# Values of the first eight sub-blocks as 64x64x64 products, and one copy for their transposed probabilities

## The chip, the cores and the metric

The kernel runs on one core of a Trainium2 chip. The metric is device time in microseconds. The engines are TensorE (PE in the profile; its weight loads are PEld), VectorE (DVE), ScalarE (ACT), GpSimd (POOL) and SyncE (SP), which issues most of the DMAs.

## The reference

Attention within chunks of 64 tokens, with 8 heads of 64, then a feed-forward layer (FFN) with a leaky relu whose slope alpha is learned per hidden unit. All of it is float32; the products of the FFN are made from a high and a low part of each operand.

```
q, k, v: (8, 8, 576, 64); chunks of 64 tokens
scores = q_c @ k_c^T / 8;  attn = softmax(scores)     # 64 x 64 per chunk and head
x = (attn @ v_c) as (4608, 512)
h = x @ w_in                                          # (4608, 2048)
g = max(h, 0) + alpha * min(h, 0)
out = g @ w_out                                       # (4608, 512)
```

## The kernel before

The 4608 tokens are 36 sub-blocks of 128 (two chunks of 64), and 9 blocks of 512. The FFN runs over blocks; the first three are computed plainly, the others in pairs with fewer products. Attention runs ahead of the FFN, a sub-block at a time, on the same engines.

The first eight sub-blocks (`s < EARLY`) make the x of blocks 0 and 1 and have a form of their own. The scores of a sub-block are eight products, one for each head, over both chunks at once: the keys stand block-diagonally in a tile with zeros elsewhere (`kbds`). A score tile has 128 partitions (the parity of the head, then 64 queries) and 512 columns (head pair, chunk, key).

- `attn_softmax` takes the maxima (L210, L212 on VectorE), eight exponentials with their sums (L217, ScalarE) and divides (L219 to L221, VectorE).
- `attn_transpose` makes four TensorE transposes of 128x128 (L245) into one PSUM bank. Its rows are then chunk and key, its columns head and query. Two ScalarE copies (L252, L253), of 64 rows each, bring chunk 0's rows into the first half and chunk 1's into the second half of a tile `pbds[s % 4]`. The other halves hold zeros, set once by eight memsets on GpSimd (L97), so the tile is block-diagonal by chunk.
- `attn_values` makes eight products (L263), one for each head: 128 rows of v by 64 columns, against 128 columns of the block-diagonal tile. They fill one bank `xo`.
- `attn_x` copies `xo` to `xh` (L295, ScalarE, rounded to the high part) and subtracts for `xl` (L296, VectorE). `done_x[s]` remembers the subtraction; the split of some weights is issued behind it.

From sub-block 8 on, scores and values are products of 64x64x64 (L194, L275), which lie on four tiles of the array and write two banks, and x comes out of these in two halves of 256 columns (L300, L301, or L291).

`attn_psum(s, n)` gives the PSUM bank: for s < 6, bank n = 1 (transposes) is `ps_o0` or `ps_o2`, bank n = 2 (values) is `ps_o1` or `ps_o3`, by the parity of s. Otherwise it is one of the two banks named `ps_a`, which all scores use too. The four `ps_o` banks later hold the FFN's second product.

The order of work: sub-blocks 0 to 3 go through scores, transpose and values as a pipeline of three stages before the FFN begins; sub-blocks 4 to 7 are written beside its first two steps. Each step is `ffn_in` for one of 16 slices f of the hidden units (L314, then L304 to L306 for the leaky relu and L326, L327 for the two parts of g) and, a step later, `ffn_out` (L339). Block 0 takes f = 0 to 2, block 1 f = 0 to 8, then each the rest; meanwhile the weights of one f after another are split into high and low parts (L130 to L138, ScalarE and VectorE). What each engine does in which order is fixed at build time by a planner that keeps dependences, has its own costs for the instructions, and prefers attention and the leaky relu (`high_priority`). A bank is given to its next user when its last reader is done.

Of the kernel before, what the change touches and what calls it, by code (L numbers as in the profile page):

```python
# [12 lines left out]
ALU = mybir.AluOpType  # L13
# [14 lines left out]
def tile_local_attention_prelu_ffn(  # L28
# [12 lines left out]
    nc = tc.nc  # L41
    P = 128
    NSUB, C = qT.shape[1], 64
    DM = out.shape[1]
    NT = NSUB * 128
    H = DM // C
# [3 lines left out]
    NP = H // 2  # L50
    SCALE = 1.0 / float(C) ** 0.5
    TB = 512
    SPB = TB // P
# [4 lines left out]
    EARLY = 2 * SPB  # L58
# [14 lines left out]
    def f32(t):  # L73
        return t.bitcast(F32)
# [4 lines left out]
    def room(n, shape):  # L79
        side, f = ("wi", NF - 1 - n // 2) if n % 2 else ("wo", NF - 1 - n // 2)  # L80
        return const.tile(shape, F32, name=f"{side}{f}")

    NBD = 4
    kbds = [room(n, [P, 2, H, C]) for n in range(NBD)]
    pbds = [room(NBD + n, [P, 2, H, C]) for n in range(NBD)]
    qs = [room(2 * NBD + n, [P, 2, H, C]) for n in range(2)]
    prs = [room(2 * NBD + 2 + n, [P, 2, H, C]) for n in range(2)]
    vs = [room(2 * NBD + 4 + n, [P, 2, DM]) for n in range(2)]
# [3 lines left out]
    for n in range(NBD):  # L92
        for c in range(2):
            (nc.vector if n == 0 else nc.gpsimd).memset(kbds[n][(1 - c) * C:(2 - c) * C, c], 0.0)
    for n in range(NBD):
        for c in range(2):
            nc.gpsimd.memset(pbds[n][(1 - c) * C:(2 - c) * C, c], 0.0)  # L97

    ident = const.tile([P, P], F32, name="ident")
    make_identity(nc, ident)  # L100
# [4 lines left out]
    def pe(ins):  # L105

        return tc.keep_in_program_order(ins) if pinned[0] else ins
# [39 lines left out]
    att = []  # L147
# [5 lines left out]
    pdiag = {}  # L153
# [12 lines left out]
    def attn_psum(s, n):  # L166
        if s < SPB + 2 and n:
            t = 2 * (s % 2) + n - 1
            return ps_o.tile([P, 512], F32, name=f"ps_o{t}")
        return ps_a.tile([P, 512], F32, name="ps_a")  # L170
# [70 lines left out]
    def attn_transpose(s):  # L241
        pr = probs.pop(s)
        tp = attn_psum(s, 1)
        for hp in range(NP):
            pe(nc.tensor.transpose(  # L245
                tp[:, hp * P:(hp + 1) * P],
                pr[:, 2 * hp:2 * hp + 2, :].rearrange("p c k -> p (c k)"),
                ident,
            ))
        tp3 = tp.rearrange("p (g k) -> p g k", k=C)  # L250
        pbd = pbds[s % NBD]
        nc.scalar.copy(pbd[0:C, 0], tp3[0:C])  # L252
        nc.scalar.copy(pbd[C:2 * C, 1], tp3[C:2 * C])  # L253
        pdiag[s] = pbd

    def attn_values(s):
        v_sb = qkv.pop(s)[2]
        p = pdiag.pop(s)
        if s < EARLY:
            xo = attn_psum(s, 2)  # L260
            for h in range(H):
                par, hp = h % 2, h // 2
                pe(nc.tensor.matmul(  # L263
                    xo[par * C:(par + 1) * C, hp * P:(hp + 1) * P],
                    lhsT=v_sb[:, h * C:(h + 1) * C],
                    rhs=p[:, :, h],
                    start=True, stop=True,
                ))
            return xo.rearrange("p (g t) -> p g t", t=P)

        for hp in range(NP):
            for par in range(2):
                for c in range(2):
                    h, rows = 2 * hp + par, slice(c * C, (c + 1) * C)
                    pe(nc.tensor.matmul(  # L275
                        att[c][par * C:(par + 1) * C, hp * C:(hp + 1) * C],
                        lhsT=v_sb[rows, h * C:(h + 1) * C],
                        rhs=p[rows, :, par * NP + hp],
                        start=True, stop=True,
                    ))  # L280
        return [a[:, :NP * C].rearrange("p (g t) -> p g t", t=C) for a in att]

    done_x = {}

    def attn_x(s, xo):
        sl = slice((s % SPB) * P, (s % SPB + 1) * P)
        if s >= PLAIN * SPB:

            for c in range(2):
                at = slice((s % SPB) * P + c * C, (s % SPB) * P + (c + 1) * C)  # L290
                nc.scalar.copy(x[s // SPB][:, :, at], xo[c])  # L291
            return
        xh, xl = x[s // SPB]
        if s < EARLY:
            nc.scalar.copy(xh[:, :, sl], xo)  # L295
            done_x[s] = nc.vector.tensor_tensor(xl[:, :, sl], xo, f32(xh[:, :, sl]), op=ALU.subtract)  # L296
            return
        for c in range(2):
            at = slice((s % SPB) * P + c * C, (s % SPB) * P + (c + 1) * C)
            nc.scalar.copy(xh[:, :, at], xo[c])  # L300
            nc.vector.tensor_tensor(xl[:, :, at], xo[c], f32(xh[:, :, at]), op=ALU.subtract)  # L301

    def prelu(g, h, f):
        nc.scalar.activation(g, h, AF.Relu, scale=-1.0)  # L304
# [85 lines left out]
    def attend(part, s):  # L390
        with tc.high_priority(offset=HIGH):
            if part == 0:
                attn_softmax(s, attn_scores(s))
            elif part == 1:
                attn_transpose(s) if s < EARLY else attn_blocks(s)
            else:
                attn_x(s, attn_values(s))

    def visit(old, new):

        att[:] = [ps_a.tile([P, TB], F32, name="ps_a") for _ in range(2)]
        with tc.high_priority(offset=HIGH):
            if old is not None:
                xo = attn_values(old)
            if new is not None:
                sc3 = attn_scores(new)
                if new + 1 < NSUB:

                    attn_load(new + 1, "q", nc.scalar)
                attn_load(new, "v")  # L410
            if new is not None:
                attn_softmax(new, sc3)
            if old is not None:
                attn_x(old, xo)
            if new is not None:
                attn_blocks(new)
# [194 lines left out]
    banks = ["ps_o0", "ps_o1", "ps_o2", "ps_o3", "ps_h", "ps_h"]  # L611
# [247 lines left out]
    for pair in range(NPAIR):  # L859
# [4 lines left out]
        g = {}  # L864
# [49 lines left out]
```

## Time and profile before

| | |
|---|---|
| median of 3 runs | 835.87 us (834.64 to 837.24) |
| the profiled execution | 835.71 us |
| its span, first to last instruction | 833.9 us |
| TensorE busy | 804.0 us, 96% |
| VectorE busy | 669.6 us, 80% |
| ScalarE busy | 548.0 us, 66% |
| GpSimd busy | 215.4 us, 26% |
| mean granted TensorE clock | 0.998 |

Busy time is the union of an engine's instructions; neighbours on one engine overlap by a little, so the time from one start to the next is often less than an instruction's own duration. In the rows below a line of the timeline is: start, length, engine, line of the kernel, operation, output and inputs by name, shape, count, and in brackets the idle time before it and what ended it. "wi" and "wo" are names of SBUF tiles: before the weights need them, these tiles hold the attention's early operands, so `ACT wo<-ps_a` is an exponential or a copy out of PSUM and not a weight.

### The profile page before, as it was taken

The numbers are of one execution on the slowest core, as the hardware profiler recorded it, in microseconds if no ns is written. First come the engines' busy times: TensorE is split into PE (matmuls) and PEld (weight loads), VectorE is DVE, ScalarE is ACT, GpSimd is POOL, SyncE is SP. The second block draws the span as 40 slices with busy tenths as digits, with TensorE's granted clock in tenths as the row PEclk, the third lists the DMA queues.
The fourth block names the chain that finished last, engine by engine and source line by source line (L and its number), as shares of the span: only waits on it lengthen the run. The fifth ranks groups of instructions, "written<-read, shape, count | busy, mean of one in ns | idle before, by whom it ended". The sixth has DMA issues, their size and how long they took to land.

```text
span 833.9 us, 15382 instructions
## 1 busy us (share of the span) xinstructions
PE 804.0 (96%) x5248; PEld 642.6 (77%) x5248; DVE 669.6 (80%) x1240; ACT 548.0 (66%) x1420; POOL 215.4 (26%) x340
## 2 busy tenths in 40 slices
PE   4799999999999999999999999999999999999998
PEld 3577888777777778778778787787887888888886
DVE  6899999987788886677779996777789965668875
ACT  5986676657666776677886555777665546566452
POOL 4006223224244431111112242111122412121232
PEclk9999999999999999999999999999999999999999
DMA  9629778657698768688876799886557995555788
GB/s 287 206 77 344 236 243 266 199 162 209 200 254 216 247 211 262 214 258 270 263 240 209 225 252 329 256 274 199 192 196 242 244 300 184 188 191 187 235 230 231
DMA packets 73966, 192.40 MB, mean 231 GB/s; under 512 B 11664, under 2 KB 19104, under 8 KB 73760
## 3 DMA queue, kind: packets, MB, share of 16 engines
q0 software_dynamic: 38272, 127.43, 49.1%
q1 hardware_dynamic: 27248, 48.91, 18.5%
q10 hardware_dynamic: 8368, 15.08, 5.7%
q8 instruction: 42, 0.69, 0.3%
q14 instruction: 36, 0.29, 0.1%
HBM read 135.27 MB, written 42.99 MB: 214 GB/s over the span
## 4 chain that ended last, share of the span: by engine, by line
PE 73%; DVE 8%; DMA 7%; ACT 6%; SPq 3%; issue 3%; ACTq 0%; DVEq 0%; POOL 0%
PE ps_o L626 17%; PE ps_o L759 14%; PE ps_h L759 12%; PE ps_h L314 9%; PE ps_o L339 9%; PE ps_h L626 8%; SPq L235 3%; DMA v_sb<-v 2%; DMA pT<-t 2%; PE ps_a L275 1%; ACT pr L217 1%; DMA wi<-kT 1%; PE ps_a L194 1%; ACT wo L217 1%; DVE gl L327 1%
## 5 line engine op out<-in xcount | busy, mean ns | idle before, releaser
L339 PE MATMUL ps_o<-wo,gh 128*128 128x512 f32 x384 | 114.5, 396 | 0.6 <-ACT more L369 0.6
L314 PE MATMUL ps_h<-xh,wi 128*128 128x512 f32 x384 | 107.0, 401 | 1.8 <-DVE g L306 1.7
L314 PEld LDWEIGHTS ps_h<-xh,wi 128*128 128x128 f32 x384 | 71.8, 190 | 20.1 <-DVE g L306 2.6
L339 PEld LDWEIGHTS ps_o<-wo,gh 128*128 128x128 f32 x384 | 71.6, 188 | 18.1 <-ACT more L369 1.0
L339 PE MATMUL ps_o<-wo,gl 128*128 128x512 f32 x192 | 69.3, 396 | 0.4 <-DVE gl L327 0.4
L626 PE MATMUL ps_o<-wi,raw 128*128 128x512 f32 x171 | 67.9, 397 | 0.0
L217 ACT ACTIVATE pr<-ps_a,mx 128x64 f32<-128x64 f32 x224 | 67.4, 327 | 0.6
L626 PE MATMUL ps_o<-wo,raw 128*128 128x512 f32 x171 | 67.8, 396 | 0.0
L314 PE MATMUL ps_h<-xl,wi 128*128 128x512 f32 x192 | 52.6, 395 | 0.0
L326 ACT CAST gh<-g 128x512 fp32r<-128x512 f32 x48 | 29.8, 621 | 29.3 <-DVE g L306 27.4
L217 ACT ACTIVATION_READ_ACCUMULATOR pr<-ps_a,mx 128x1 f32 x224 | 48.9, 218 | 0.0
L564 POOL DMA_DIRECT2D raw<-wi_a x42 | 22.4, 535 | 102.1 <-PE ps_o L626 61.7
L304 ACT ACTIVATE wo<-gh 128x512 f32<-128x512 f32 x24 | 15.2, 634 | 51.1 <-DVE gh L649 51.1
L582 ACT CAST gh<-wi 128x512 fp32r<-128x512 f32 x45 | 28.0, 623 | 25.2 <-PE ps_o L759 10.9
L564 POOL DMA_DIRECT2D raw<-wo_a x42 | 22.4, 534 | 84.7 <-PE ps_o L759 43.9
L339 PEld LDWEIGHTS ps_o<-wo,gl 128*128 128x128 f32 x192 | 35.9, 188 | 9.6 <-DVE gl L327 0.8
L314 PEld LDWEIGHTS ps_h<-xl,wi 128*128 128x128 f32 x192 | 36.0, 188 | 8.5
L304 ACT ACTIVATE g<-ps_h 128x512 f32<-128x512 f32 x48 | 29.3, 611 | 18.3 <-PE ps_h L314 16.9
L626 PE MATMUL ps_o<-wi,wo 128*128 128x512 f32 x99 | 39.3, 397 | 0.0
L626 PE MATMUL ps_o<-wo,wo 128*128 128x512 f32 x99 | 39.1, 395 | 0.0
L626 PEld LDWEIGHTS ps_o<-wo,raw 128*128 128x128 f32 x171 | 32.2, 188 | 7.7
L626 PEld LDWEIGHTS ps_o<-wi,raw 128*128 128x128 f32 x171 | 32.1, 188 | 7.6
(252 smaller groups left out, 2280.9 us busy)
## 6 DMA issues: line engine op xcount, KB each, us to landing
raw<-wi_a POOLq DMA_DIRECT2D x42, 512.0 KB, 4.8
raw<-wo_a POOLq DMA_DIRECT2D x42, 512.0 KB, 4.1
wi<-wi_a POOLq DMA_DIRECT2D x21, 512.0 KB, 4.5
wo<-wi_a POOLq DMA_DIRECT2D x21, 512.0 KB, 4.8
wi<-wo_a POOLq DMA_DIRECT2D x21, 512.0 KB, 3.8
wo<-wo_a POOLq DMA_DIRECT2D x21, 512.0 KB, 4.3
v_sb<-v SPq DMA_DIRECT2D x28, 256.0 KB, 4.5
pT<-t SPq DMA_DIRECT2D x224, 32.0 KB, 3.9
```

The source lines that it names most:

```text
L194: pe(nc.tensor.matmul(att[par][c * C:(c + 1) * C, (NP + hp) * C:(NP + hp + 1) * C], lhsT=q_sb[rows, 2 * hp + c], rhs=kb[rows, 2 * hp + c], ...
L217: last = nc.scalar.activation(pr[:, g], one, AF.Exp, bias=mx[:, g], scale=SCALE, accum_out=sm[:, g])
L235: nc.sync.dma_start(out=pT[dst, i].rearrange("p h t -> p (h t)"), in_=tb[src, j].rearrange("p h t -> p (h t)"),)
L275: pe(nc.tensor.matmul(att[c][par * C:(par + 1) * C, hp * C:(hp + 1) * C], lhsT=v_sb[rows, h * C:(h + 1) * C], rhs=p[rows, :, par * NP + hp ...
L304: nc.scalar.activation(g, h, AF.Relu, scale=-1.0)
L314: pe(nc.tensor.matmul(hps, lhsT=wi[f][:, l, k * P:(k + 1) * P], rhs=xx[:, k], start=(i == 0 and k == 0), stop=(i == 2 and k == NK - 1),))
L326: nc.scalar.copy(gh, g)
L339: pe(nc.tensor.matmul(o, lhsT=a[:, ts], rhs=wo[f][:, l], start=(f == first and i == 0), stop=(f == last and i == 2),))
L564: streamed[0] = nc.gpsimd.dma_start(out=f32(t), in_=units[side][n])
L582: hi = nc.scalar.copy(t_hi, t)
L626: pe(nc.tensor.matmul(ps, lhsT=w[:, l, k * P:(k + 1) * P], rhs=xx[:, xl], start=first and at == 0, stop=at == n - 1, skip_group_check=not ...
L759: pe(nc.tensor.matmul(ps[m], lhsT=w[:, l, m * P:(m + 1) * P], rhs=xx, start=i != 6 and j == 0 and n == 0, stop=j == JF - 1 and n == 2, ski ...
```

## The change

For the first eight sub-blocks, the transposed probabilities leave PSUM in one copy of 128 rows by 512 columns, into the first half of the same tile, which is no longer block-diagonal; the eight memsets go. The values become sixteen products of 64x64x64, as in the later sub-blocks: chunk c takes 64 rows of v and of the probabilities, and writes to a bank of its own. The two banks are n = 2 as before and n = 1, the one that held the transposes. x is then made in two halves, one for each chunk, by the same lines as in the later sub-blocks of the first three blocks; `done_x[s]` is the second half's subtraction.

```
-    pbds = [room(NBD + n, [P, 2, H, C]) for n in range(NBD)]
+    pTs = [room(NBD + n, [P, 2, H, C]) for n in range(NBD)]
...
-    for n in range(NBD):
-        for c in range(2):
-            nc.gpsimd.memset(pbds[n][(1 - c) * C:(2 - c) * C, c], 0.0)
...
-        tp3 = tp.rearrange("p (g k) -> p g k", k=C)
-        pbd = pbds[s % NBD]
-        nc.scalar.copy(pbd[0:C, 0], tp3[0:C])
-        nc.scalar.copy(pbd[C:2 * C, 1], tp3[C:2 * C])
-        pdiag[s] = pbd
+        pT = pTs[s % NBD][:, 0]
+        nc.scalar.copy(pT, tp.rearrange("p (h t) -> p h t", t=C))
+        pdiag[s] = pT
...
-        if s < EARLY:
-            xo = attn_psum(s, 2)
-            for h in range(H):
-                par, hp = h % 2, h // 2
-                pe(nc.tensor.matmul(
-                    xo[par * C:(par + 1) * C, hp * P:(hp + 1) * P],
-                    lhsT=v_sb[:, h * C:(h + 1) * C],
-                    rhs=p[:, :, h],
-                    start=True, stop=True,
-                ))
-            return xo.rearrange("p (g t) -> p g t", t=P)
+        early = s < EARLY
+
+        banks = [attn_psum(s, n) for n in (2, 1)] if early else att

         for hp in range(NP):
             for par in range(2):
                 for c in range(2):
                     h, rows = 2 * hp + par, slice(c * C, (c + 1) * C)
                     pe(nc.tensor.matmul(
-                        att[c][par * C:(par + 1) * C, hp * C:(hp + 1) * C],
+                        banks[c][par * C:(par + 1) * C, hp * C:(hp + 1) * C],
                         lhsT=v_sb[rows, h * C:(h + 1) * C],
-                        rhs=p[rows, :, par * NP + hp],
+                        rhs=p[rows, h] if early else p[rows, :, par * NP + hp],
                         start=True, stop=True,
                     ))
-        return [a[:, :NP * C].rearrange("p (g t) -> p g t", t=C) for a in att]
+        return [a[:, :NP * C].rearrange("p (g t) -> p g t", t=C) for a in banks]
...
-        if s < EARLY:
-            nc.scalar.copy(xh[:, :, sl], xo)
-            done_x[s] = nc.vector.tensor_tensor(xl[:, :, sl], xo, f32(xh[:, :, sl]), op=ALU.subtract)
-            return
         for c in range(2):
             at = slice((s % SPB) * P + c * C, (s % SPB) * P + (c + 1) * C)
             nc.scalar.copy(xh[:, :, at], xo[c])
-            nc.vector.tensor_tensor(xl[:, :, at], xo[c], f32(xh[:, :, at]), op=ALU.subtract)
+            done_x[s] = nc.vector.tensor_tensor(xl[:, :, at], xo[c], f32(xh[:, :, at]), op=ALU.subtract)
```

More of the change, by code (lines that the diff above doesn't have):

```diff
@@ L275, in attn_values @@
                     pe(nc.tensor.matmul(
-                        att[c][par * C:(par + 1) * C, hp * C:(hp + 1) * C],
+                        banks[c][par * C:(par + 1) * C, hp * C:(hp + 1) * C],
                         lhsT=v_sb[rows, h * C:(h + 1) * C],
-                        rhs=p[rows, :, par * NP + hp],
+                        rhs=p[rows, h] if early else p[rows, :, par * NP + hp],
                         start=True, stop=True,
                     ))
-        return [a[:, :NP * C].rearrange("p (g t) -> p g t", t=C) for a in att]
+        return [a[:, :NP * C].rearrange("p (g t) -> p g t", t=C) for a in banks]
     done_x = {}
     def attn_x(s, xo):
-        sl = slice((s % SPB) * P, (s % SPB + 1) * P)
         if s >= PLAIN * SPB:
```

## The prediction

> **What bounds the kernel now.** I read the page's busy shares first, then a table by stage, then the chain of work inside the stage that the change touches.
>
> ```profile
> PE 804.0 (96%) x5248; PEld 642.6 (77%) x5248; DVE 669.6 (80%) x1240; ACT 548.0 (66%) x1420; POOL 215.4 (26%) x340
> ```
>
> Over the whole span TensorE (PE) is the bound, but the first eight sub-blocks lie in the first 62 us, so the stages decide. The columns after the stretch are its length, then the busy time of each engine.
>
> ```profile
> core 0: us, PE busy (x) PEld busy (x) DVE busy (x) ACT busy (x) POOL busy (x), PEclk, DMA share, GB/s
> 13.67:36.76 23.09, 14.05 (x172) 10.67 (x168) 19.89 (x49) 22.90 (x101) 0.00 (x0) 0.97 0.84 265
> 36.76:62.00 25.24, 25.24 (x150) 19.53 (x151) 22.00 (x48) 20.67 (x61) 0.00 (x0) 0.96 0.25 83
> 62.00:80.00 18.00, 16.81 (x73) 13.29 (x72) 17.84 (x36) 11.27 (x20) 12.09 (x17) 1.00 0.95 334
> 80.00:140.00 60.00, 60.00 (x260) 48.38 (x259) 57.03 (x117) 38.69 (x66) 15.95 (x21) 1.00 0.79 254
> ```
>
> There are four stages with four different bounds. From 13.67 us to the first matmul of the FFN at 36.76 us ScalarE (ACT) is busy 22.90 of 23.09 us. From there to 62 us PE never stops. From 62 to 80 us VectorE (DVE) is full, 17.84 of 18.00, and PE has its only gap. After 80 us PE is full again, so a microsecond won there is kept. The chain that ends at the first FFN matmul says the same of the first stage:
>
> ```profile
> 16.57 0.59 ACT wo L252
> ...
> 17.17 0.59 ACT wo L253
> ...
> 17.78 2.48 ACT wi L217 x16
> ...
> 36.76 0.79 PE ps_h L314
> ```
>
> Every step of it up to 36.7 us is ACT: the exponentials (L217), the two copies that bring transposed probabilities into the diagonal blocks (L252, L253), the copy that makes xh (L295), and the weights' casts. What ACT no longer does there, PE starts earlier.
>
> **The change part by part.**
>
> *One copy for two (ACT, on the path).* A pair of 64x512 copies becomes one copy of 128x512. The same columns pass per partition, only more partitions. How much the pairs hold before and after 36.76 us:
>
> ```profile
> 13.67:36.76 23.09, 2.96 (x5) 0.97 0.84 265
> 13.67:36.76 23.09, 2.91 (x5) 0.97 0.84 265
> L369 ACT COPY wo<-ps_o 128x512 f32<-128x512 f32 x2 | 1.2, 606 | 0.0
> ```
>
> The first row is L252 alone, the second L253 alone: five pairs (sub-blocks 0 to 4) lie before the FFN's start. The third is the nearest row to the new copy, 128x512 from PSUM at 0.606 us; it takes what one 64-row copy takes (2.96 / 5 = 0.59). So each pair saves about 0.58 us; five save 2.96 + 2.91 - 5 x 0.606 = 2.84 us on the path. The other three pairs lie in the stage where ACT has 4.6 us to spare and are worth nothing directly.
>
> *xh in two halves (ACT, on the path).* One 128x512 cast becomes two of 128x256. Later blocks already do this:
>
> ```profile
> 30.34 0.64 ACT L295 CAST xh<-ps_o 128x512 fp32r<-128x512 f32 x1
> 30.81 0.60 ACT L252 COPY wi<-ps_o 64x512 f32<-64x512 f32 x1
> ...
> 189.61 0.69 ACT L300 CAST xh<-ps_a 128x256 fp32r<-128x256 f32 x2
> 190.12 0.80 ACT L305 ACTIVATE g<-g,alpha_sb 128x512 f32<-128x512 f32 x1
> ```
>
> From start to next start the whole cast holds ACT 0.47 us (30.34 to 30.81) and the two halves together 0.51 (189.61 to 190.12). Neighbours overlap, so busy times would overstate it: by union 0.69 against 0.64. The price is +0.04 us each, at worst (no overlap with what follows) 0.69 - 0.47 = +0.22. Four casts lie before the FFN's start: +0.2, at worst +0.9. Net on ACT: -2.84 + 0.2 = -2.6 us, bounds -2.84 and -1.9. The first FFN matmul moves from 36.76 to about 34.1.
>
> *xl in two halves (DVE).*
>
> ```profile
> 53.92 0.68 DVE L296 TENSOR_TENSOR xl<-ps_a,xh 128x512 fp32r<-128x512 f32 x1
> 54.52 0.42 DVE L131 TENSOR_SCALAR t<-t 128x512 f32<-128x512 f32 x1
> ...
> 190.21 0.42 DVE L301 TENSOR_TENSOR xl<-ps_a,xh 128x256 fp32r<-128x256 f32 x1
> 190.66 0.37 DVE L301 TENSOR_TENSOR xl<-ps_a,xh 128x256 fp32r<-128x256 f32 x1
> ```
>
> The whole subtraction holds DVE 0.60 us (53.92 to 54.52), two halves between 0.66 and 0.79 (0.42 + 0.37). That is +0.06 to +0.19 each; I take +0.1, so 0.4 us in the first stage and 0.8 us over all eight. DVE covers this where it waits on ACT, and its waits before 62 us are these:
>
> ```profile
> DVE sm L219 <- ACT wi L217: 4.0, 4, 1.7
> DVE sm L219 <- ACT wo L217: 1.0, 2, 0.7
> ```
>
> Those 5.0 us are waits for the exponentials. When ACT runs 0.5 us ahead per sub-block, they shrink and DVE gets ahead too, but only by the idle time it has. That matters because 62 to 80 us belongs to DVE: PE can arrive there 2.6 us earlier and gain only what DVE has gained. I take 2.6 us for DVE's lead (the waits exceed it), less its extra 0.8 us: -1.8, and -0.2 more as some of that 0.8 falls in idle time. So -2.0 us survive at 80 us. Bounds: nothing, if DVE gives up no idle time, to -2.6.
>
> *Values in 64x64x64 pieces (PE).* Eight products with 128 columns become sixteen with 64; each shows as two passes.
>
> ```profile
> 51.93 1.09 PE L263 MATMUL ps_a<-wo,wi 128*64 128x128 f32 x16
> 52.95 0.96 PE L339 MATMUL ps_o<-wo,gl 128*128 128x512 f32 x3
> ...
> 158.14 0.69 PE L194 MATMUL ps_a<-k_sb,q_sb 64*64 64x64 f32 x32
> 158.77 1.20 PE L314 MATMUL ps_h<-xh,wi 128*128 128x512 f32 x4
> ```
>
> The old set holds PE 1.02 us (51.93 to 52.95), sixteen 64x64x64 products 0.63 (158.14 to 158.77), although they are 32 passes. That is 0.39 us less for each. Sub-blocks 0 to 4 ran in a stage where PE idles 9 us: nothing. Sub-blocks 5 to 7 lie where PE is full: -1.2 us, and there DVE's full stage behind takes it back, so I count none of it.
>
> *Second bank (waits).* The values now also fill the bank that held the transpose, ps_o0 or ps_o2, and free it only with the last xl half. So transpose s+2 waits for xl of s. In the old order:
>
> ```profile
> 30.70 0.63 PE L245 MATMUL ps_o<-ident,wo 128*128 128x128 f32 x4 [0.17 <-DVE wo L221]
> 32.34 0.68 DVE L296 TENSOR_TENSOR xl<-ps_o,xh 128x512 fp32r<-128x512 f32 x1
> 33.78 0.58 ACT L252 COPY wo<-ps_o 64x512 f32<-64x512 f32 x1
> ```
>
> Transpose 4 ran at 30.70, while xl of sub-block 2 ended at 33.02. Only the copy at 33.78 needs that transpose, so a wait until 33.02 (+0.63) still fits almost; behind it in PE's queue stand the values of sub-block 3, from which the FFN's first operand is made. The planner knows the bank and can place xl earlier (xh of 2 was done at 30.98). I take zero; the upper end is 33.02 - 30.70 = 2.3 us. For sub-blocks 6 and 7 the values need both ps_a banks, so they wait until the exponentials of 7 have left theirs: at most one softmax, 2.48 us by the row at 17.78, hidden while PE has FFN work that may go first.
>
> *No zeros (POOL).*
>
> ```profile
> L97 POOL MEMSET wi<- x4: 518/612/706, 5.2 to 8.6; 64x512 f32 x4
> ```
>
> The last of the eight starts at 8.6 us and ends before 9.4; behind them on POOL stand the identity and the load of alpha, which move forward by eight times 0.5 to 0.7 us. The chain before 13.67 us runs through the second K load, and that is bound by the DMA:
>
> ```profile
> 2.71 7.83 DMA wi<-kT
> ```
>
> It lands at 10.54, later than the memsets end. Worth 0; the cover is this load, and without it they would cost at most 8 x 0.6 = 4.9 us.
>
> **Sum.** Profiled time 835.71 (span 833.9, with 1.8 around it), 0.16 under the median 835.87. ACT -2.84 + 0.2, DVE takes 0.6 of it, PE and POOL 0: -2.0 us, so 833.7 against the profiled run and 833.9 against the median. A measurement of this kernel can tell about 0.3%, 2.5 us, from no change; the forecast lies inside that, near its edge.
>
> **Rivals.**
>
> *The whole gain and more (faster).* At the start of the FFN PE runs at half clock:
>
> ```profile
> 35.40:38.40 3.00, 2.89 (x18) 2.20 (x15) 1.67 (x4) 3.00 (x17) 0.00 (x0) 0.50 0.76 255
> ```
>
> ```profile
> 35.01 1.64 PE L263 MATMUL ps_o<-wo,wo 128*64 128x128 f32 x16 [1.86 <-DVE t L136]
> ```
>
> The granted clock (the column after POOL) is 0.50 until 38.4; from 36.76 on that costs 0.8 us. If the earlier start falls outside such a stretch, and DVE follows ACT in full, the sum is -2.6 - 1.2 (values 5 to 7) - 0.8 = -4.6: 831.3. Against it: less PE work before the FFN makes a cold start as likely as a warm one, and DVE is full at 62 us. The Trainium skill ("TensorE: Matmul & The Clock Gate", Part 1) says that about 3.4 us of idling throttles the clock; the idle stretch before this one was 1.86 us, so by the rule alone the slow stretch should not be there and the forecast would be 0.8 us lower; the trace decides.
>
> *The gain is absorbed (no change).* DVE keeps its pace, because its raw weights are split at the same times, or transpose 4's wait (up to 2.3 us) takes it back. Sum 0 to +0.3: 836. For it: 17.84 of 18 us. Against: 5.0 us of DVE's waits were for ACT.
>
> *Changes of the array's shape (slower).* PE already mixes three shapes where values 5, scores 7 and transposes 6 are ready together:
>
> ```profile
> 43.81 0.27 PE L245 MATMUL ps_a<-ident,wi 128*128 128x128 f32 x1
> 44.01 0.43 PE L180 MATMUL ps_a<-wi,wi 128*64 128x128 f32 x2
> 44.37 0.33 PE L245 MATMUL ps_a<-ident,wi 128*128 128x128 f32 x1
> 44.63 0.43 PE L180 MATMUL ps_a<-wi,wi 128*64 128x128 f32 x2
> ...
> 46.91 0.27 PE L263 MATMUL ps_o<-wi,wo 128*64 128x128 f32 x1
> 46.91 0.38 PE L180 MATMUL ps_a<-wi,wi 128*64 128x128 f32 x2
> ```
>
> A transpose and two score passes repeat every 0.62 us (44.01 to 44.63), where three such passes in one shape take 3 x 0.064 = 0.19 (1.02 / 16 each): two changes cost 0.43, so about 0.2 each. L180 and L263 alternated one by one at no cost, since both were 128x64. With 64x64 pieces each alternation is a change: up to 32, 6.4 us. From 13 of them the gain is gone, from about 23 the kernel is slower by over 2.5 us; at the full count 835.9 - 2.0 + 6.4 = 840.3, at 25 of them 838.9. Against it: values and scores need not be ready together again, and late blocks run them one after the other. The Trainium skill ("TensorEngine Tiling (Array Packing)", Key Properties) states that changing the tiling mode drains TensorE; by that rule this rival holds wherever shapes alternate, and the 0.62 us period agrees.
>
> **How the numbers follow.** Forecast 0.45, own range 832.4 to 835.3; whole gain 0.22 (831 to 833); absorbed 0.20 (835.3 to 837); shape changes 0.13 (837 to 840). Faster by over 0.3% (below 833.4): 0.22 and a third of 0.45, 0.37. Slower (above 838.4): most of the last and little else, 0.12. Within: 0.51. The range leaves a tenth out at each end: 831.4 to 838.0.
>
> **What would show it.** Right: eight ACT copies of 128x512 near 0.6 us; xh in pairs of 128x256; the first FFN matmul near 34 us; DVE's waits on the exponentials under 4 us; PE's gap after 62 us larger than 1.2. Wrong: the first FFN matmul later than 36 us, transposes 2 to 4 waiting for xl, L263's pieces alternating with L180 at about 0.2 us each, or a half-clock stretch longer than 3 us.

## The result, and the profile after

The changed kernel is slower: 841.25 us median (837.87 to 844.7, 17 runs) against 837.16 us (834.2 to 839.86, 17 runs) for the kernel before, run beside it. The ratio is 1.0052, with an interval of 1.0037 to 1.0067, so 3 to 6 us. The profiled execution took 843.9 us (span 842.1), which is near the slow end of its 17 runs: the two profiled executions are 8.2 us apart, the medians 4.1.

The page after, first part: busy time, share and instructions of each engine.

```profile
PE 810.8 (96%) x5376; PEld 647.0 (77%) x5376; DVE 668.0 (79%) x1248; ACT 543.8 (65%) x1420; POOL 215.1 (26%) x332
```

ScalarE does 4.2 us less. TensorE, whose new value sets are shorter, is busy 6.8 us longer than before. The new copy is as long as was predicted; these are its four lines by tile:

```profile
L248 ACT COPY wo<-ps_o x3: 586/613/615, 17.1 to 41.1; 128x512 f32<-128x512 f32 x3
L248 ACT COPY wi<-ps_o x3: 585/587/683, 20.9 to 42.0; 128x512 f32<-128x512 f32 x3
L248 ACT COPY wo<-ps_a x1: 585/585/585, 46.4 to 46.4; 128x512 f32<-128x512 f32 x1
L248 ACT COPY wi<-ps_a x1: 588/588/588, 59.5 to 59.5; 128x512 f32<-128x512 f32 x1
```

Eight copies of about 0.6 us, as long as one 64-row copy was. Two stages of the table by stage (columns as before: length, busy time of PE, PEld, DVE, ACT, POOL, then the granted clock) show where the gain did not arrive:

```profile
13.67:36.76 23.09, 14.63 (x221) 11.71 (x218) 20.14 (x56) 21.06 (x107) 0.00 (x0) 0.75 0.83 253
36.76:62.00 25.24, 24.27 (x184) 18.23 (x184) 15.97 (x40) 14.32 (x47) 0.00 (x0) 0.89 0.17 56
```

ScalarE, full before (22.90), now has two idle microseconds in the first stage, so it no longer sets the FFN's start alone. In the second stage VectorE does 15.97 us of work where it did 22.00, although all that work is still to be done. The timeline of TensorE (start, length, line, operation, passes, and in brackets the idle time before) has the steps of interest:

```profile
26.87 0.63 PE L242 MATMUL ps_o<-ident,wi 128*128 128x128 f32 x4 [0.93 <-DVE xl L283]
...
36.43 0.80 PE L296 MATMUL ps_h<-xh,wi 128*128 128x512 f32 x1 [1.87 <-ACT xh L282]
...
44.22 0.27 PE L242 MATMUL ps_a<-ident,wi 128*128 128x128 f32 x1
44.42 0.43 PE L177 MATMUL ps_a<-wi,wi 128*64 128x128 f32 x2
44.78 0.33 PE L242 MATMUL ps_a<-ident,wi 128*128 128x128 f32 x1
...
50.37 0.32 PE L262 MATMUL ps_o<-wi,wo 64*64 64x64 f32 x4
50.62 0.72 PE L296 MATMUL ps_h<-xl,wi 128*128 128x512 f32 x2
...
56.86 1.20 PE L296 MATMUL ps_h<-xh,wi 128*128 128x512 f32 x4 [0.96 <-ACT wi L131]
```

The transpose of sub-block 2 (L242) waits for xl of sub-block 0; the FFN starts at 36.43, not 34.1; from 44.22 to 50.62 single transposes, scores and values alternate; at 56.86 the FFN waits for weights. The waits of all engines from 13.67 to 62 us name what else was late:

```profile
DVE g L288 <- ACT g L287: 6.0, 1, 6.0
...
ACT xh L282 <- PE ps_o L262: 3.0, 2, 2.7
...
PE ps_h L296 <- ACT wi L131: 1.0, 1, 1.0
```

VectorE stood idle for 6.0 us. In the planner's order the next things it does are x of sub-block 4 (48.13) and, behind it, the split of the weights of the third FFN slice (f = 2). The first row is the start of that split before, the others are VectorE's timeline after:

```profile
40.78 0.42 DVE L131 TENSOR_SCALAR t<-t 128x512 f32<-128x512 f32 x1
```

```profile
45.32 0.69 DVE L288 SCALAR_TENSOR_TENSOR g<-ps_h,g 128x512 f32<-128x512 f32 x1 [6.00 <-ACT g L287]
...
48.13 0.75 DVE L283 TENSOR_TENSOR xl<-ps_o,xh 128x256 fp32r<-128x256 f32 x2
48.80 0.41 DVE L128 TENSOR_SCALAR t<-t 128x512 f32<-128x512 f32 x1
...
57.95 0.68 DVE L135 SCALAR_TENSOR_TENSOR wi<-t,t 128x512 fp32r<-128x512 uint32 x1
```

The split began at 48.80 instead of 40.78 us. So the planner's order is a different one, and the loss can be dated by counting FFN matmuls (`ffn_in` and `ffn_out`, counted from 0 in order of start). In before's order number 72 is the first of block 1; in after's it is number 60. Starts in us, out of the traces; the runs e6 to e18 are described below:

| FFN matmul | 0 | 12 | 24 | 36 | 60 | 72 | 96 |
|---|---|---|---|---|---|---|---|
| before | 36.8 | 41.0 | 47.5 | 50.4 | 57.6 | 61.7 | 68.6 |
| after | 36.4 | 42.8 | 52.1 | 56.9 | 64.6 | 67.5 | 73.4 |
| e6, before, after's order | 37.9 | 43.2 | 51.9 | 56.5 | 64.5 | 67.6 | 73.2 |
| e7, all changed, sets whole in before's order | 35.4 | 38.8 | 43.8 | 46.6 | 53.4 | 61.3 | 70.0 |
| e8, before, sets whole | 37.1 | 41.0 | 46.3 | 49.2 | 56.3 | 60.4 | 66.1 |
| e9, as e7, last two sub-blocks early | 35.4 | 40.3 | 45.3 | 48.2 | 56.0 | 59.5 | 65.9 |
| e11, as e7, 6 and 7 unchanged | 35.9 | 39.3 | 44.2 | 47.1 | 54.5 | 58.6 | 64.1 |
| e14, as e7, 4 to 7 unchanged | 38.2 | 41.5 | 46.7 | 49.6 | 56.8 | 60.9 | 66.5 |
| e15, as e11, after's order of sets | 34.9 | 38.6 | 45.7 | 50.1 | 59.9 | 62.8 | 68.4 |
| e16, as e11, two copies | 39.9 | 44.8 | 49.8 | 53.2 | 60.5 | 64.8 | 71.4 |
| e18, as e15, weights of f = 2 earlier | 34.0 | 39.3 | 44.7 | 48.7 | 54.8 | 61.2 | 68.5 |

After lies 0.3 us ahead at the start, 4.6 behind at matmul 24, 6.5 at 36 and 4.8 at 96. From there to 140 us the distance stays within 0.5 us of that; so a loss of the size of the medians' is made between 36 and 73 us, where sub-blocks 4 to 7 run beside the FFN.

The table does not reach further. From matmul 96 to the end, work that the edits do not touch took 765.3 us in before's profiled execution, 768.7 in after's, and between 762 and 771 in those of the experiments below. A difference of a few microseconds between two medians is therefore placed in this stage only as far as the table shows it there.

### The profile page after: what moved, and what is told of

Same layout as the page of the kernel before. It is cut to its first block, busy times and chain, and to the rows that moved or that the text cites. A ratio compares the mean times of both kernels' runs of the same rounds, so it can differ in the third digit from the quotient of the medians.

```text
span 842.1 us, 15630 instructions
## 1 busy us (share of the span) xinstructions
PE 810.8 (96%) x5376; PEld 647.0 (77%) x5376; DVE 668.0 (79%) x1248; ACT 543.8 (65%) x1420; POOL 215.1 (26%) x332
## 3 DMA queue, kind: packets, MB, share of 16 engines
q0 software_dynamic: 38272, 127.43, 48.2%
## 4 chain that ended last, share of the span: by engine, by line
PE 62%; DMA 12%; DVE 11%; ACT 6%; SPq 4%; issue 4%; POOL 1%; ACTq 0%; DVEq 0%; POOLq 0%
PE ps_o L608 15%; PE ps_o L741 14%; PE ps_h L741 11%; PE ps_h L608 8%; PE ps_h L296 6%; PE ps_o L321 5%; SPq L232 3%; DMA pT<-t 2%; ACT pr L214 2%; DMA wi_a<-raw 2%; DMA more<-w_in 2%; DMA v_sb<-v 1%; DMA k_sb<-kT 1%; PE ps_a L262 1%; DVE g L288 1%
## 5 line engine op out<-in xcount | busy, mean ns | idle before, releaser
L321 PE MATMUL ps_o<-wo,gh 128*128 128x512 f32 x384 | 116.4, 400 | 0.0
L286 ACT ACTIVATE wo<-gh 128x512 f32<-128x512 f32 x24 | 15.2, 634 | 51.8 <-DVE gh L631 51.8
L321 PEld LDWEIGHTS ps_o<-wo,gl 128*128 128x128 f32 x192 | 36.5, 190 | 9.4 <-DVE gl L309 0.6
L309 DVE TENSOR_TENSOR gl<-g,gh 128x512 fp32r<-128x512 f32 x48 | 32.8, 684 | 8.4 <-ACT gh L308 7.9
L608 PE MATMUL ps_o<-wi,wo 128*128 128x512 f32 x99 | 39.3, 397 | 0.0
L288 DVE SCALAR_TENSOR_TENSOR g<-ps_h,g 128x512 f32<-128x512 f32 x48 | 32.6, 681 | 8.4 <-ACT g L287 8.4
```

The costliest lines, as they stand in the source:

```text
L288: nc.vector.scalar_tensor_tensor(g, in0=h, scalar=0.0, in1=g, op0=ALU.max, op1=ALU.subtract)
L309: low = nc.vector.tensor_tensor(gl, g, f32(gh), op=ALU.subtract)
L321: pe(nc.tensor.matmul(o, lhsT=a[:, ts], rhs=wo[f][:, l], start=(f == first and i == 0), stop=(f == last and i == 2),))
L608: pe(nc.tensor.matmul(ps, lhsT=w[:, l, k * P:(k + 1) * P], rhs=xx[:, xl], start=first and at == 0, stop=at == n - 1, skip_group_check=not ...
```

## The experiments

All times are medians; a ratio is to the kernel before in the same group of runs (836.8 to 837.8 us), and differences between groups go by the ratios. The theories: **A**, the pieces' changes of the array's shape beside the FFN; **B**, the second bank and the half clock before it; **C**, the planner's order; **D**, the pieces cost it in any order; later **E** (alternation and the second ps_a bank of the last sub-blocks) and **F** (late weights). Where an edit has `new_form`, the eight memsets stay, and the new copies go to four tiles of their own.

**e1 and e2: the change in half of the sub-blocks.**

```
+    def new_form(s):
+        return s < SPB
...
-        if s < EARLY:
+        if s < EARLY and not new_form(s):
```

(e2: `SPB <= s < EARLY`.)

> The change in sub-blocks 0 to 3 alone; 4 to 7 keep the diagonal tile, the zeros and the 128-column products. Theory A (shape changes of the array beside the FFN's first steps cost the time): the planner's order has as many changes of shape after the FFN's start as before (13, against 22 in the changed kernel), so no loss: within 1.5 us of before, with the copies' gain up to 2 us faster. Theory B (the second bank delays transposes 2 to 4, and a prologue with less and later TensorE work keeps the clock at half when the FFN starts): all of that is in here, so 3 to 5 us slower than before, with the first FFN matmul not earlier than 36 us.

> The change in sub-blocks 4 to 7 alone; 0 to 3 as before. Theory A: 27 changes of shape after the FFN's start against 13 before, at 0.19 us each about 2.7 us slower than before, up to 4. Theory B: the prologue up to the first FFN matmul is as before, so within 1 us of before.

Measured: e1 843.11, 1.0065 (1.0044 to 1.0087); e2 838.09, 1.0015 (0.9997 to 1.0033). Sub-blocks 0 to 3 carry the whole loss, though only the others run beside the FFN. A alone is out. B had the direction, but not its sign: in e1 the FFN started at 35.7 us, not later than before.

**e3: the changed kernel, sets from values 4 on chained one behind the other on TensorE.**

```
+        behind = tc.issue_after(tail[0].ins) if tail[0] and (part + s >= 6 and s >= SPB) else nullcontext()
+        with tc.high_priority(offset=HIGH), behind:
```

> The changed kernel with one thing added: from values 4 on, each set of early attention products (scores, transposes, values of a sub-block) is queued on TensorE behind the whole set before it, so that sets no longer alternate product by product. 12 changes of shape after the FFN's start in place of 22. Theory A: at least 10 x 0.19 = 1.9 us faster than the changed kernel, about 838 to 839.5. Theory B: no faster than the changed kernel, 840.5 to 842.

Measured: 843.36, 1.0074 (1.0049 to 1.01). It is no faster than the changed kernel, as B said. FFN matmul 48 came 17.8 us after matmul 0 (after: 23.8), but sub-block 7 came late and gave all of it back.

**e4: the kernel before with x in two halves, nothing else.**

```
+            for c in range(2):
...
+                nc.scalar.copy(xh[:, :, at], half)
+                done_x[s] = nc.vector.tensor_tensor(xl[:, :, at], half, f32(xh[:, :, at]), op=ALU.subtract)
```

> The kernel before with x made in two halves (two ScalarE casts and two VectorE subtractions of 256 columns for each early sub-block) and nothing else. Both theories: +0.04 us on ScalarE and +0.1 on VectorE for each sub-block, so within 1 us of before. Should it be 2 us or more slower, the halves, or a new order of the planner by itself, would explain the loss without A or B.

Measured: 840.79, 1.0046 (1.0031 to 1.006): neither theory foresaw it, and it pointed to the order, theory C.

**e5 to e8: the order written out.** A chain of ordering edges (no waits) puts TensorE's early instructions in a given order; the planner orders all the rest anew. S, T, V are scores, transposes and values of a sub-block, F0.1 is `ffn_in` of block 0, f = 1; a count takes so many of a set.

```
+    def in_turn():
+        last = None
+        for token in TURN.split():
+            what, _, count = token.partition(":")
+            for _ in range(int(count) if count else len(made[what])):
+                ins = made[what].pop(0)
+                if last is not None:
+                    tc.add_manual_dep(ins, last.name, NOSYNC, reason="in_turn")
+                last = ins
```

e7 (changed) and e8 (before) have whole sets: `S0 S1 S2 T0 S3 V0 T1 S4 T2 V1 V2 S5 T3 S6 T4 V3 V4 F0.0:4 F0.1:4 T5 F0.0 F0.1 T6 S7 V5 F0.2 V6 T7 V7 F1.0 F1.1`. e5 (changed) is the same with T6, S7 and V5 alternating as before's planner had them. e6 (before) has after's order: `... V0 T1 V0 S4 V1 S5 T2 T3 S6 V2 V3 F0.0:4 F0.1:4 T4 T5 ...`, with its alternation.

> The changed kernel whole, with TensorE's instructions of the eight early sub-blocks (scores, transposes, values) and of the FFN's first steps chained in the order in which the kernel before has them, each piece of a value set in place of its half. Theory C (the loss of 4 us lies in the order that the planner chose for the changed kernel: transposes 2 to 5 and scores 6 later, sub-block 7 and the weights of f=2 and 3 later): 835 to 838 us, and the 96th FFN matmul starts within 1 us of the kernel before's 68.6. Rival D (pieces, halves and the second bank cost it in any order): 840.5 to 844, 96th matmul at 72 or later.

> The kernel before, none of its instructions changed, with TensorE's order of sets and their alternation chained as in the changed kernel (its value sets of 8 in the places of the 16 pieces). Theory C: 840 to 844 us, the 96th FFN matmul at 72 or later. Rival D: 836 to 838, the 96th matmul within 1.5 us of 68.6.

> The changed kernel with the order of the sets of the kernel before, and no alternation of single instructions: each set stands whole on TensorE. Theory C with a price of the alternation of about 0.2 us for each change of shape: 833.5 to 836.5. Rival D: 839 to 843.

> The kernel before with its own order of sets, but each set whole on TensorE (6 of 13 changes of shape after the FFN's start are gone). Both theories: 835 to 837; at about 0.2 us for each change it gains 1.2, if the time of those matmuls is on the path. It is the measure for the run before it: theory C has the two within 1.5 us of each other, rival D has the changed kernel 3 us or more behind.

Measured: e5 844.56, 1.0085 (1.0066 to 1.0105); e6 841.03, 1.0036 (1.0022 to 1.0051); e7 839.93, 1.0027 (1.0011 to 1.0044); e8 836.13, 0.9986 (0.9968 to 1.0004). Order alone costs before 3 us (e6), as C said, and from matmul 12 to 96 e6's starts are within 0.5 us of after's: the kernel before, with none of its instructions changed, then runs late where after does. But before's order does not rescue the changed kernel (e5, e7), as D said. Each explains a part. Alternation is priced by e5 against e7, the same three sets on TensorE. e5:

```profile
42.81 0.27 PE L245 MATMUL ps_a<-ident,wi 128*128 128x128 f32 x1
43.01 0.43 PE L180 MATMUL ps_a<-wi,wi 128*64 128x128 f32 x2
43.37 0.33 PE L245 MATMUL ps_a<-ident,wi 128*128 128x128 f32 x1
...
48.11 0.33 PE L265 MATMUL ps_o<-wi,wo 64*64 64x64 f32 x4
48.37 0.74 PE L299 MATMUL ps_h<-xh,wi 128*128 128x512 f32 x2
```

e7:

```profile
41.58 0.60 PE L245 MATMUL ps_a<-ident,wi 128*128 128x128 f32 x4
42.10 1.09 PE L180 MATMUL ps_a<-wi,wi 128*64 128x128 f32 x16
43.13 0.69 PE L265 MATMUL ps_o<-wi,wo 64*64 64x64 f32 x32
43.75 1.20 PE L299 MATMUL ps_h<-xh,wi 128*128 128x512 f32 x4
```

5.56 us against 2.17: 18 changes of shape (transposes and FFN have the same) against 3, 3.39 / 15 = 0.23 us each. The Trainium skill ("TensorEngine Tiling (Array Packing)", Key Properties) says that a change of the tiling mode drains TensorE; the price that these rows show agrees with it, though they do not show what the time goes to. Then, in e7, the lead of 4.2 us at matmul 60 is lost at one blow:

```profile
47.65 0.33 PE L265 MATMUL ps_a<-wo,wi 64*64 64x64 f32 x2
...
52.74 0.69 PE L265 MATMUL ps_a<-wo,wi 64*64 64x64 f32 x30
...
56.26 0.60 PE L245 MATMUL ps_a<-ident,wi 128*128 128x128 f32 x4
58.35 0.69 PE L265 MATMUL ps_a<-wi,wi 64*64 64x64 f32 x32 [1.49 <-ACT wi L251]
61.28 1.20 PE L299 MATMUL ps_h<-xh,wi 128*128 128x512 f32 x2 [2.24 <-ACT xh L285]
```

Values 6 start at 47.65 and cannot go on: their second ps_a bank holds the scores of 7. They end at 53.4, transpose 7 and values 7 follow, and TensorE runs out of work twice, 1.49 and 2.24 us. After that the clock is halved for 3.4 us. That is theory E.

**e9 to e12: the last two sub-blocks, and the halves.** e9 (changed) and e10 (before): the order of e7 up to V5, then `F0.2:8 G0.0 V6 F0.2:4 G0.1:4 T7 G0.1:8 V7 G0.2 F1.0 F1.1` (G is `ffn_out`). e11: e7 with `new_form(s)` = `s < 6`, so values 6 and 7 take one bank. e12: e4 in e8's order.

> The changed kernel, all its pieces and banks, with its sets whole in the order of the kernel before up to values 5, and then chained so that the last two sub-blocks come early: values 6, transposes 7 and values 7 among the first ffn_out's, ahead of the rest of them. Theory E (the pieces and the one copy do save 3 to 4 us up to the 48th FFN matmul; it is lost again to the alternation, and to values 6, which need a second ps_a bank, wait for exps 7 to leave it and hold transpose 7 back behind the subtraction of x 6, after which TensorE runs out of work at 57 to 61 us and then gets half the clock): 831 to 834.5 us, the 72nd FFN matmul (the first of block 1) at 56 to 58.5, the 96th at 62.5 to 66, no wait of TensorE over 1 us between 44 and 66. Rival D (pieces, halves and banks cost it in any order): 837 to 841.

> The kernel before with the order of the run before this one. Theory E: TensorE has work all the way from the FFN's start to the 96th matmul in the kernel before, so that an earlier sub-block 7 gives it nothing: 834.5 to 837 us, the 96th matmul at 65.5 to 67.5; the changed kernel in the same order is 2 to 4 us ahead of it. Rival D: the changed kernel is behind it by 2 us or more.

> The earlier run of the changed kernel in the order of before with whole sets, and one edit: sub-blocks 6 and 7 keep the values of the kernel before (one bank, blocks of 64x128, two copies). Theory E: values 6 no longer wait for exps 7 (they stand whole at about 48 us, not at 53) and transpose 7 not for the subtraction of x 6; first matmul of block 1 at 58 to 60.5 and not 61.3; 836 to 838.5 us, against 839.9. Rival D, and any cause outside the last two sub-blocks: no change, 839 to 841.

> The kernel before with x in two halves, as in the earlier run that lost 4 us, but with its own order of sets chained whole. Theory E (that loss came from the order alone, the FFN's start at 41.6 us): 834.5 to 837.5 us, within 1.2 of the kernel before in whole sets (836.1); FFN's start at 36.5 to 38. Rival (the halves cost it by themselves, through ScalarE and VectorE): 839 or more.

Measured: e9 835.32, 0.9973 (0.9955 to 0.9991); e10 836.36, 1.0001 (0.9985 to 1.0018); e11 831.98, 0.9935 (0.9917 to 0.9953); e12 842.43, 1.0068 (1.0042 to 1.0093). e9 missed its range by 0.8 us and its matmul 72 by 1 us (59.5), but it beats before; in the same order the changed kernel is ahead by 0.0028, about 2 us. e11 gained more than expected: by the ratios 7.7 us against e7, of which 5.9 stand in the table at matmul 96, with values 6 whole at 48.16:

```profile
48.16 1.09 PE L275 MATMUL ps_a<-wo,wi 128*64 128x128 f32 x16
...
53.94 0.60 PE L253 MATMUL ps_a<-ident,wi 128*128 128x128 f32 x4
...
56.51 1.09 PE L275 MATMUL ps_a<-wi,wi 128*64 128x128 f32 x16
57.54 1.20 PE L353 MATMUL ps_o<-wo,gl 128*128 128x512 f32 x4
58.57 1.08 PE L328 MATMUL ps_h<-xh,wi 128*128 128x512 f32 x4
```

(The last three rows are values 7, the rest of `ffn_out`, and block 1, with no gap.) e12 went against E: 842 us, the FFN's start at 40.5. There the second cast of a sub-block comes behind VectorE's subtraction of the first half, which reads the same bank, and other work stands between the casts: those of sub-block 3 start at 38.90 and 40.03. The next run tests this.

**e13 to e16: what was left open.** e13: e12 with both casts ahead of both subtractions. e14: `new_form(s)` = `s < SPB` in e7's order. e15: e11 in after's order of sets, whole: `S0 S1 S2 T0 S3 V0 T1 S4 V1 S5 T2 T3 S6 V2 V3 F0.0:4 F0.1:4 T4 T5 F0.0 F0.1 T6 S7 V4 V5 F0.2 V6 T7 V7`. e16: e11 with `ffn_out` chained in e11's place too, and

```
+            nc.scalar.copy(pTs[s % NBD][0:C, 0], tp3[0:C])
+            nc.scalar.copy(pTs[s % NBD][C:2 * C, 0], tp3[C:2 * C])
```

> The kernel before in its own order with whole sets, x in two halves out of its one bank, but both casts ahead of both subtractions, so that the second cast waits for TensorE alone. Theory E (the earlier runs with halves lost their 4 to 5 us in the wait of the second cast for VectorE's subtraction of the first half, which the changed kernel with its two banks does not have): 835 to 837.5 us, FFN's start at 36.5 to 38. Rival (twice the casts and subtractions cost it): 839 or more.

> The change in sub-blocks 0 to 3 alone, which lost 6 us as the planner ordered it, with the sets whole and in the order of the kernel before. Theory E: 832 to 835.5 us, FFN's start at 35 to 36.5, the 96th FFN matmul at 64.5 to 67. Rival (the second bank of the first four, for which transposes 2 to 5 wait, costs it in any order): 838 or more, FFN's start later than 37.

> The version with the change in sub-blocks 0 to 5 that ran at 832.0, with whole sets, but in the order of sets that the planner chose for the changed kernel (values 1 and scores 5 ahead of transposes 2 and 3, values 2 and 3 ahead of the FFN, transposes 4 and 5 behind its first 8 matmuls). If the order of the sets has a price of its own: 834 to 838 us. Rival (alternation and the ps_a bank are all of the loss): 830.5 to 833.5.

> The version that ran at 832.0, with the transposed probabilities of sub-blocks 0 to 5 leaving PSUM in two copies of 64 partitions, same order on TensorE. If ScalarE's second copy is on the path to the FFN's start, as the prediction had it: five times 0.58, FFN's start at 37.3 to 39 and not 35.9, 833.5 to 836 us. Rival (TensorE's shorter value sets made the gain, ScalarE has slack): FFN's start within 0.7 of 35.9, 831 to 833.

Measured: e13 833.41, 0.9962 (0.9947 to 0.9977); e14 831.73, 0.9945 (0.9926 to 0.9964); e15 841.22, 1.0052 (1.0033 to 1.0072); e16 839.04, 1.0022 (1.0009 to 1.0034). Halves cost nothing when the casts stand together (that e13 is even faster than e8 is not explained: its matmul 96 is at 66.9, 0.8 later).

The form of e1 gains 4.6 us in a good order, so e1's loss was order. But e14 missed its expected start (35 to 36.5) and showed the sign of the rival, a start later than 37: 38.2, behind e8's 37.1, although four of its second copies are gone. Its transposes 3 and 4 wait for xl of sub-blocks 1 and 2, as the second bank has it:

```profile
30.52 0.66 PE L253 MATMUL ps_o<-ident,wi 128*128 128x128 f32 x4 [1.74 <-DVE xl L315]
...
33.96 0.63 PE L253 MATMUL ps_o<-ident,wo 128*128 128x128 f32 x4 [1.76 <-DVE xl L315]
...
38.15 2.12 PE L328 MATMUL ps_h<-xh,wi 128*128 128x512 f32 x8 [1.06 <-ACT xh L314]
```

At matmul 96 it is 2.1 us ahead of before and 0.4 behind e8; the rest of its gain lies behind, and is not explained.

After's order of sets costs 9 to 10 us against e11 (e15), though its FFN starts at 34.9. In the profiled executions 4.3 us of that are there at matmul 96 (68.4 and 64.1), and some 3 more come between matmuls 250 and 300, where e15 waits for g:

```profile
116.31 1.20 PE L328 MATMUL ps_h<-xh,wi 128*128 128x512 f32 x4 [2.51 <-DVE g L320]
```

And two copies cost 7 us (e16): its FFN starts 4 us later. ScalarE's timeline, at the first exponential of sub-block 5, in e16 and then in e11:

```profile
33.90 0.31 ACT L225 ACTIVATE wo<-ps_a,mx 128x64 f32<-128x64 f32 x1 [1.07 <-DVE mx L220]
```

```profile
30.24 0.41 ACT L225 ACTIVATE wo<-ps_a,mx 128x64 f32<-128x64 f32 x1
```

That is 3.7 us by then, more than the busy time of the four extra copies so far (2.3). Part of it is a wait of 1.07 us for VectorE's maxima, which e11 does not have. The other part is that a second copy costs more than its busy time. From start to next start a pair held ScalarE 1.21 us before (16.57 to 17.78 in the prediction's chain); the single copy in e11 holds it 0.48:

```profile
24.82 0.59 ACT L260 COPY wo<-ps_o 128x512 f32<-128x512 f32 x1
25.30 0.31 ACT L225 ACTIVATE wo<-ps_a,mx 128x64 f32<-128x64 f32 x1
```

So the copies are on the path, and the path runs through VectorE too.

**e17 and e18: weights of f = 2 behind x 3 instead of x 4**, in the changed kernel and in e15.

```
-            prepare(ready, done_x.get({2: SPB, 3: SPB + 2, 4: SPB + 3}.get(ready)))
+            prepare(ready, done_x.get({2: SPB - 1, 3: SPB + 2, 4: SPB + 3}.get(ready)))
```

> The changed kernel with one edit: the weights of f=2 are split behind the x of sub-block 3 and no longer behind that of sub-block 4 (the planner orders the rest anew). Theory F (the second bank moves transpose 4, with it x 4, and with that the weights of f=2, which TensorE then waits for): the halves of both weights of f=2 are ready by 52 us and not at 61.4, no wait of TensorE for them; 835.5 to 839.5 us. Rival (the loss is the alternation of single instructions and the second ps_a bank): 840 or more.

> The version with the planner's order of sets, whole, and the change in sub-blocks 0 to 5 (841.2 us), with the same one edit: weights of f=2 behind x 3. Theory F: the 60th FFN matmul at 54 to 57 us and not 59.9; 833 to 837 us. Rival (the order costs it in another way, as by x 4 to x 7 themselves): 839 or more.

Measured: e17 846.29, 1.0106 (1.0086 to 1.0127); e18 834.88, 0.9983 (0.9965 to 1.0001). By its numbers F holds without alternation: one edit takes back 5.8 us by the ratios, and matmul 60 starts at 54.8, 5.1 us earlier than in e15. But the table does not place the gain there. e18's profiled execution waits 2.4 us for x 7 at matmul 72, and at matmul 96 it is level with e15 (68.5 and 68.4); e15 falls behind later, at the wait at 116.31 above and after it. So earlier weights move the middle of this stage, and what the 5.8 us come from is not shown. These are VectorE's rows where the split begins in e15, behind x 4, and where its first weight is done in e18:

```profile
45.20 0.75 DVE L315 TENSOR_TENSOR xl<-ps_o,xh 128x256 fp32r<-128x256 f32 x2
45.86 0.42 DVE L139 TENSOR_SCALAR t<-t 128x512 f32<-128x512 f32 x1
```

```profile
40.56 0.68 DVE L146 SCALAR_TENSOR_TENSOR wi<-t,t 128x512 fp32r<-128x512 uint32 x1
```

In the changed kernel itself (e17) the weights were early too (42.3 and 44.4 us), and it lost 4.5 us more: the planner alternated even longer (45.4 to 51.8 us without a pause) and x 7 came at 68. There the weights are not the bound.

## Why the prediction was wrong

The forecast was 833.9 us, 2.0 below the kernel before; the changed kernel took 841.25, 4.1 above the 837.16 measured beside it. All four signs named as "wrong" came: FFN later than 36 us, a transpose waiting for xl, values alternating with scores, a half clock longer than 3 us.

- **One copy for two: on the path, and worth more than was said, but only in an unchanged order.** The copy takes 0.6 us as forecast. The sum took busy times for the pair; from start to next start a pair saves 1.21 - 0.48 = 0.73 us and not 0.58, so five save 3.7 us and not 2.84. That is near the 3.9 us by which e16 starts its FFN later than e11. In the changed kernel the FFN starts 0.3 us earlier than before.
- **Halves of xh and xl: right.** Nothing measurable (e13). The edit that seemed to say otherwise (e4, e12) had a wait that two banks do not have.
- **Shorter value sets: right in size** (0.62 us for 32 passes against 1.02).
- **Second bank counted at zero, 2.3 us at most: this is the step that failed, in two places.** For sub-blocks 0 to 3, the sum read the wait off the old order ("Transpose 4 ran at 30.70 ... a wait until 33.02"). Where that order is kept, the wait is there and is not zero: transposes 3 and 4 wait 1.67 and 1.02 us for xl in e7, 1.74 and 1.76 in e11, and not at all in e8; and e16, which has two copies as e8 has, starts its FFN 2.8 us later than e8 (the pieces and the planner's new order on the other engines are in that too). In the changed kernel the planner did not keep that order: it moved transposes 2 and 3 behind values 1, and 4 and 5 behind the FFN's first matmuls. Values 4 fell behind the FFN's first slices, x 4 came 8 us later, and with it the weights of f = 2. That order by itself, alternation included, makes the kernel before 3 us slower and gives it after's starts (e6); with the change in sub-blocks 0 to 5 and whole sets it costs 4.3 us by matmul 96 and 9 to 10 in all (e15 against e11). How much of it those weights cost is not shown (e18). For sub-blocks 6 and 7, "at most one softmax, 2.48 us, hidden while PE has FFN work" left out who stands behind: transpose 7, values 7, block 1. e7's trace shows the waits (1.49 and 2.24 us, then half the clock). The old form of these two sub-blocks, with its one bank, is 7.7 us faster where the rest goes well (e11 against e7); the bank was not changed apart from the rest of that form.
- **The rival of shape changes had the right price and too small a chance.** It said 0.2 us; measured 0.23. (Its "from 13 of them the gain is gone" should be 10, by its own 2.0 and 0.2 us.) The order after has 22 such changes behind the FFN's start (up to 110 FFN matmuls), before's 13. In after the alternating stretch takes 6.40 us, where the same passes whole take about 3.1 (e7's sets, values 4 and half of values 6 added); before lost 1.3 that way (3.74 against 2.42 in e8). So it is 2 us of the 4.8, not all.
- **Half clock, taken as 0.8 us of chance.** Before, it lasted until 38.82 us (the prediction read 38.4, the end of the stretch that it had asked for), which cost 1.0 us from the FFN's start on. After, it held from 28.4 to 42.1 us, which cost half of 42.08 - 36.43, 2.8 us: 1.8 more.

So of the 4.9 us that after loses between FFN matmuls 0 and 24, the clock has 1.8 and the alternation 2.0; about as much as is left would be the sets that stood ahead of the FFN before, transpose 4 and values 4 (0.52 and 0.62 by e7's rows). From 24 to 36, where values 6 and the weights of f = 2 are waited for, it loses 1.9 more, and gets 1.7 back by 96.

What stays open: the parts are priced in chained orders, and the planner orders ScalarE and VectorE anew each time, so they do not add up to the loss of the changed kernel to the microsecond. Nor is it known what makes the work behind matmul 96 take up to 8 us more in one version than in another. No single repair that was tried in the changed kernel was enough there: neither earlier weights (e17), nor whole sets (e3), nor before's order (e5, e7); whole sets in that order with the last two sub-blocks early were (e9, 0.9973).

The two fastest versions are e14 (the change in sub-blocks 0 to 3) at 0.9945 and e11 (0 to 5) at 0.9935, about 5 us under the kernel before, both with the order written out and sets whole.

## What to carry to other kernels

Where a planner rebuilds the order, a change that gives a buffer a second user is a change of the order: before summing durations, ask which instruction must now come later, what is queued behind it on each engine (here the split of weights behind x 4), and price that, not the wait in the old order. Compare the two planned orders by counting one engine's work in sequence; a table of the k-th matmul's start dates a loss faster than busy shares, but follow it to the end of the span before a gain in the total is put down to the stage that was edited. When a good edit loses, chain the old order on the new instructions and the new order on the old ones: the two runs part the instructions from their order.

## What the runs showed of the hardware

The clock goes by a fixed grid. In every trace its changes lie whole multiples of 3.413 us apart, to 0.002 us, and they go with how busy TensorE was in the grid's last window. After (length, busy PE, ..., granted clock):

```profile
18.19:21.60 3.41, 1.16 (x24) 0.72 (x14) 3.13 (x10) 3.41 (x18) 0.00 (x0) 1.00 1.04 287
21.60:25.01 3.41, 3.27 (x52) 2.85 (x54) 1.57 (x4) 3.12 (x20) 0.00 (x0) 0.50 1.04 317
25.01:28.43 3.42, 1.55 (x20) 1.10 (x16) 3.42 (x12) 3.42 (x20) 0.00 (x0) 1.00 1.06 298
28.43:31.84 3.41, 2.30 (x16) 2.00 (x18) 3.41 (x11) 2.19 (x9) 0.00 (x0) 0.50 0.75 262
```

A window with 1.16 or 1.55 us of matmuls is followed by half clock; in the kernel before one with 1.86 is not, and one with 1.48 is:

```profile
28.57:31.99 3.42, 1.86 (x22) 1.27 (x20) 3.18 (x10) 3.41 (x11) 0.00 (x0) 1.00 0.48 189
31.99:35.40 3.41, 1.48 (x24) 1.24 (x26) 2.98 (x7) 3.35 (x18) 0.00 (x0) 1.00 0.36 80
```

(The granted clock of a row is that of the window itself; what it leads to shows in the next one, for the last row the half clock from 35.40.) Between 14 and 820 us of the 20 traces the clock fell 47 times, 46 of them behind a window in which TensorE was busy 50% or less (the other: 54%); only five windows under 50% were not followed by a fall, all of them at 47 to 49%. At half clock, 47 windows with 86% or more brought full clock back, and 14 with 82% or less did not. The Trainium skill ("TensorE: Matmul & The Clock Gate", Part 1) gives the grid of 3413 ns, which agrees, and asks for an idle window before the clock falls; here a half busy one is enough. So shorter matmuls in a stage that another engine bounds can cost the clock of the next window: this was not tried by itself.
